# Four V-gradient stores of a decode layer go as GpSimd scatters that skip partitions 36 to 39, with those rows in a four-row SyncE store

## The chip, the cores and the metric

One core of a Trainium2 chip. The metric is device microseconds (us) of that core. A time is the median of a kernel's runs, with the lowest and highest in brackets. The span on a profile page is the profiled run's own, and is some 2 us shorter than the time of the same run. All runs of both kernels, and all timed runs of the experiments, were in the fast state, so all the comparisons below are of fast runs. One experiment (the probe) was run once, so its state is unknown, and its time is not used.

## The reference, cut to what matters

The kernel computes the forward and the backward pass of one decode layer. The layer adds, to its input, an attention over a long cache and a gated MLP.

```python
def _A_ref(x, k_cache, v_cache, wq, wo):           # x: 1 x 1 x 640
    q = transpose((x @ wq).reshape(B, Sq, 32, 128))
    scores = einsum("bhqd,bhkd->bhqk", q, k_cache) * 128 ** -0.5   # caches: 1 x 32 x 8192 x 128, bf16
    o = einsum("bhqk,bhkd->bhqd", softmax(scores), v_cache)
    return transpose(o).reshape(B, Sq, 32 * 128) @ wo
...
return x + _A_ref(layernorm(x), ...) + _B_ref(layernorm(x), ...)   # _B_ref: SwiGLU, F = 1728
# outputs: the layer's out, and the gradients of x, k_cache, v_cache, wq, wo, w1, w3, w2
```

The two caches have 67 MB each, and so have their gradients dK and dV. Everything else is small. Reading K and V and writing dK and dV is nearly all of the 303.9 MB that the core moves.

## The kernel before

A head's K or V is one 2 MB tile: 128 partitions, 16 KB in each. There are ten slots for such tiles. The gradient is written over the tile, and the tile is then stored. All loads and stores of these tiles go through one helper, on one queue, that of SyncE, which issues them in program order:

```python
dvc = out_3.rearrange("b h (p j) d -> (b h) p (j d)", p=P)     # dV, one 128-row block for each head
...
def fifo(out_, in_):                    # L102 of the profile
    nc.sync.dma_start(out_, in_)
...
free_slots = [kvpool.tile([P, KVN], BF16, name=f"kv{i}", tag=f"kv{i}") for i in range(NSLOT)]  # 10 slots
def load_next():
    if not pending or len(free_slots) < lag[0]:
        return
    kind, h = pending.pop(0)
    t = free_slots.pop(0)
    fifo(t[:], (kc if kind == "K" else vc)[h])
    kv_tiles[(kind, h)] = t
...
lag[0] = 3                              # a load goes into the slot that was stored three stores back
...
def store(kind, h):
    t = kv_tiles.pop((kind, h))
    if kind == "K":
        hd.pop(h)
    fifo((dkc if kind == "K" else dvc)[h], t[:])
    free_slots.append(t)
    load_next()
```

A load has to wait until the store that last used its slot has landed. Because the queue is in order, every wait of SyncE holds back all that stands behind it. Most of the projection weights, their gradients and those of the MLP go through the GpSimd queue, which moves 26.3 of the 303.9 MB.

## Time and profile before

| | before |
|---|---|
| time, us | 735.03 (734.04 to 735.35), 4 runs |
| span of the profiled run, us | 733.2 |
| TensorE (PE) busy | 608.6 us, 83% |
| moved | 303.90 MB, mean 414 GB/s |
| last tile store: sixteenth part lands after the fifteenth by | 8.06 us |

The page of the kernel before: busy time of the engines; DMA busy share in tenths and GB/s in 40 slices of 18.3 us; and the tile transfers with their count, size and median us from issue to landing.

```profile
PE 608.6 (83%) x5663; PEld 425.9 (58%) x5663; DVE 461.1 (63%) x806; ACT 367.9 (50%) x716; POOL 30.0 (4%) x45
...
DMA  9999999999999999999999999999999999999993
GB/s 337 401 410 420 425 428 423 400 421 422 417 422 426 429 427 424 427 430 426 429 425 428 429 420 427 429 429 427 425 428 427 428 432 428 428 431 429 422 390 154
...
out_dram<-kv SPq DMA_DIRECT2D x64, 2048.0 KB, 31.0
kv<-in_A_k_cache_dram SPq DMA_DIRECT2D x32, 2048.0 KB, 25.1
kv<-in_A_v_cache_dram SPq DMA_DIRECT2D x32, 2048.0 KB, 26.3
```

The DMA engines bound this kernel. They run at 417 to 432 GB/s in nearly every slice between the third and the last two, while the busiest compute engine is idle 17% of the time. Packet by packet, the trace shows sixteen chains ("lanes" below), one for each DMA engine. Each moves one 16 KB row after another, in 0.611 us (median), and 16 rows are in flight nearly all the time from 10 to 695 us. The table of transfers explains why: a 2 MB transfer is 4.9 us of work at 427 GB/s, yet it takes 25 to 31 us from issue to landing. So five or so transfers stand in the queue at any moment.

Busy time by stretch of the kernel before. The columns are: stretch; its length; busy us of PE, PE weight load, VectorE, ScalarE and GpSimd with their instructions in brackets; TensorE's granted clock; DMA share; GB/s.

```profile
276.00:288.00 12.00, 11.48 (x123) 8.26 (x125) 8.84 (x17) 7.89 (x17) 1.65 (x2) 0.99 1.00 421
366.00:378.00 12.00, 11.15 (x116) 7.93 (x115) 7.78 (x10) 8.06 (x16) 0.00 (x0) 1.00 1.02 425
...
544.00:556.00 12.00, 10.13 (x101) 7.16 (x101) 5.53 (x14) 7.46 (x16) 0.77 (x1) 0.86 1.00 425
715.00:720.00 5.00, 0.56 (x2) 0.50 (x2) 4.00 (x20) 0.00 (x0) 0.86 (x1) 0.50 0.84 340
...
725.00:733.00 8.00, 0.00 (x0) 0.00 (x0) 0.00 (x0) 0.00 (x0) 0.00 (x0) 0.50 0.05 23
```

In the middle of the run the DMA share is 1 (all sixteen lanes always have a packet). At the end it is not: in the last 8 us it is 0.05, which is one lane of sixteen, at 23 GB/s. A transfer lands in sixteen parts, one for each lane, and one lane has fallen behind the others by 8.06 us when the last tile store lands. That lane alone sets the end. This is the slack that the change is after. (A head's V is stored before its K, so the last store of all is dK of head 31, issued at 710.13 us. The recorded texts call it the last V store. The last V store proper is issued at 705.73, and its gap is 8.53 us in before and 4.80 in after.)

A number used below is *lost time*: the length of a stretch less the megabytes moved in it divided by 427 GB/s, the full rate. For before it is 8.05 us from 0 to 150 us (start-up), 0.25 us from 150 to 696 us, and 13.19 us from 696 us to the end.

SyncE's issues in a part of the kernel before (start; us; line and operation), and what SyncE waited for in the whole run (us in total, times, longest):

```profile
253.58 0.33 SPq L102 DMA_DIRECT2D kv<-in_A_v_cache_dram  x1
255.90 0.34 SPq L102 DMA_DIRECT2D out_dram<-kv  x1
263.62 0.33 SPq L102 DMA_DIRECT2D kv<-in_A_k_cache_dram  x1
266.96 0.34 SPq L102 DMA_DIRECT2D out_dram<-kv  x1
```

```profile
SPq L102 <- DMA out_dram<-kv: 458.2, 54, 17.1
```

SyncE waits most of the time, for stores to land, and this costs nothing: it is silent for up to 12.5 us between two issues in the middle of the run, and the queue has more work than that.

### The profile page before, as it was taken

The numbers are of one execution on the slowest core, as the hardware profiler recorded it, in microseconds if no ns is written. First come the engines' busy times: TensorE is split into PE (matmuls) and PEld (weight loads), VectorE is DVE, ScalarE is ACT, GpSimd is POOL, SyncE is SP. The second block draws the span as 40 slices with busy tenths as digits, with TensorE's granted clock in tenths as the row PEclk, the third lists the DMA queues.
The fourth block names the chain that finished last, engine by engine and source line by source line (L and its number), as shares of the span: only waits on it lengthen the run. The fifth ranks groups of instructions, "written<-read, shape, count | busy, mean of one in ns | idle before, by whom it ended". The sixth has DMA issues, their size and how long they took to land.

```text
span 733.2 us, 13850 instructions
## 1 busy us (share of the span) xinstructions
PE 608.6 (83%) x5663; PEld 425.9 (58%) x5663; DVE 461.1 (63%) x806; ACT 367.9 (50%) x716; POOL 30.0 (4%) x45
## 2 busy tenths in 40 slices
PE   1998579998899889988999797888698888899840
PEld 1666457666666666665666565555475566666520
DVE  4059655677766666667767755646746576477482
ACT  1650726665465455655565554545464455554510
POOL 0010010000100000000000000000000000000000
PEclk9996699999899889988899988989989799888965
DMA  9999999999999999999999999999999999999993
GB/s 337 401 410 420 425 428 423 400 421 422 417 422 426 429 427 424 427 430 426 429 425 428 429 420 427 429 429 427 425 428 427 428 432 428 428 431 429 422 390 154
DMA packets 27428, 303.90 MB, mean 414 GB/s; under 512 B 2836, under 2 KB 4436, under 8 KB 10724
## 3 DMA queue, kind: packets, MB, share of 16 engines
q1 hardware_dynamic: 21328, 276.39, 89.3%
q0 software_dynamic: 5728, 26.30, 8.9%
q8 instruction: 44, 0.72, 0.4%
q10 hardware_dynamic: 308, 0.33, 0.1%
q14 instruction: 20, 0.16, 0.1%
HBM read 151.67 MB, written 151.34 MB: 413 GB/s over the span
## 4 chain that ended last, share of the span: by engine, by line
PE 42%; DMA 41%; ACT 7%; DVE 7%; issue 2%; SPq 0%; ACTq 0%; DVEq 0%
PE pT L294 19%; DMA kv<-in_A_k_cache_dram 18%; DMA out_dram<-kv 17%; PE m L329 6%; PE X L406 5%; ACT KT L296 4%; DMA kv<-in_A_v_cache_dram 4%; PE sA L313 3%; PE dA L313 2%; DVE kv L439 2%; DMA wo_g<-in_A_wo_dram 2%; ACT kv L589 1%; PE gu_ps L516 1%; DVE side L240 1%; ACT KT L319 1%
## 5 line engine op out<-in xcount | busy, mean ns | idle before, releaser
L296 ACT COPY KT<-pT 128x512 f32<-128x512 f32 x512 | 290.4, 590 | 235.7 <-PE pT L294 204.3
L294 PE MATMUL pT<-ident_f,kv 128*128 128x128 f32 x2048 | 321.8, 298 | 36.5 <-DMA kv<-in_A_k_cache_dram 27.3
L294 PEld LDWEIGHTS pT<-ident_f,kv 128*128 128x128 f32 x2048 | 251.7, 156 | 93.2 <-PE pT L294 29.5
L439 DVE TENSOR_TENSOR kv<-qd,U 128x4096 bf16<-128x4096 bf16 x64 | 146.1, 2285 | 0.0
L439 DVE TENSOR_TENSOR kv<-qd,P 128x4096 bf16<-128x4096 bf16 x64 | 143.6, 2285 | 0.0
L329 PEld LDWEIGHTS m<-selc,KT 128*128 128x128 f32 x512 | 67.6, 206 | 47.1 <-ACT KT L319 37.4
L329 PE MATMUL m<-selc,KT 128*128 128x16 f32 x512 | 73.7, 277 | 24.4 <-ACT KT L319 24.2
L406 PE MATMUL X<-kv,Z 128*32 128x512 bf16 x1024 | 84.9, 460 | 1.8 <-DVE Z L423 1.8
L389 DVE SCALAR_TENSOR_TENSOR U<-m,P 128x64 bf16<-128x64 f32 x32 | 7.4, 233 | 105.4 <-PE m L329 105.4
L313 PE MATMUL sA<-KT,qz 128*32 128x512 bf16 x512 | 55.4, 423 | 0.0
L313 PE MATMUL dA<-KT,qz 128*32 128x512 bf16 x512 | 54.5, 412 | 0.2 <-ACT KT L296 0.2
L313 PEld LDWEIGHTS <-qz 128*32 128x32 bf16 x1024 | 26.5, 93 | 42.7 <-issue 41.6
L406 PEld LDWEIGHTS <-Z 128*32 128x32 bf16 x1024 | 28.7, 110 | 34.0 <-issue 17.0
L355 DVE TENSOR_REDUCE mrow<-m 128x1 f32<-128x64 f32 x32 | 7.2, 224 | 60.9 <-PE m L329 60.9
L349 ACT CAST qd<-pT 128x256 bf16<-128x256 f32 x32 | 11.9, 373 | 49.3 <-DVE kv L439 31.6
L489 DVE SCALAR_TENSOR_TENSOR wq_g<-wq_g,side 128x512 bf16<-128x512 bf16 x40 | 27.3, 683 | 0.0
L240 DVE SCALAR_TENSOR_TENSOR side<-wo_g,g_bc 128x640 bf16<-128x640 bf16 x32 | 26.2, 820 | 1.4 <-DMA wo_g<-in_A_wo_dram 1.0
L362 DVE TENSOR_REDUCE negM<-m 128x1 f32<-128x128 f32 x32 | 9.3, 292 | 25.2 <-PE m L359 25.2
L421 DVE SCALAR_TENSOR_TENSOR U<-m,P 128x128 bf16<-128x128 f32 x32 | 11.4, 355 | 19.3 <-PE m L419 19.3
L379 DVE RECIPROCAL rZ<-m 128x1 f32<-128x1 f32 x32 | 5.3, 167 | 24.2 <-PE m L373 24.2
L319 ACT COPY KT<-dA 128x512 f32<-128x512 f32 x32 | 19.4, 605 | 0.6 <-PE dA L313 0.6
L319 ACT COPY KT<-sA 128x512 f32<-128x512 f32 x32 | 19.3, 602 | 0.0
(143 smaller groups left out, 363.2 us busy)
## 6 DMA issues: line engine op xcount, KB each, us to landing
out_dram<-kv SPq DMA_DIRECT2D x64, 2048.0 KB, 31.0
kv<-in_A_k_cache_dram SPq DMA_DIRECT2D x32, 2048.0 KB, 25.1
kv<-in_A_v_cache_dram SPq DMA_DIRECT2D x32, 2048.0 KB, 26.3
out_dram<-wo_g POOLq DMA_DIRECT2D x8, 640.0 KB, 12.0
out_dram<-wq_g POOLq DMA_DIRECT2D x8, 640.0 KB, 13.0
wq_g<-in_A_wq_dram POOLq DMA_DIRECT2D x7, 640.0 KB, 13.2
wo_g<-in_A_wo_dram POOLq DMA_DIRECT2D x7, 640.0 KB, 19.5
kv<-in_B_w_dram SPq DMA_DIRECT2D x2, 1728.0 KB, 27.1
```

Source lines behind the costliest of these rows:

```text
L240: nc.vector.scalar_tensor_tensor(junk[:], G_["wo"][:, hh, :], 1.0, g_bc[:], ALU.mult, ALU.mult, accum_out=G_["do"][:, hh:hh + 1])
L294: nc.tensor.transpose(pT[:, k * P:(k + 1) * P], W3[:, 4 * c + k, :], ident_f[:])
L296: nc.scalar.copy(KT[:].rearrange("p k w -> p (k w)"), pT[:])
L313: nc.tensor.matmul(S_[kind][q:q + QW, :], lhsT=S_["qz"][:, o:o + QW], rhs=KTb[:, par, :], start=(c0 == 0), stop=(c0 == NCH - 2), skip_grou ...
L319: nc.scalar.copy(XS[:].rearrange("p k w -> p (k w)"), S_.pop(kind)[:])
L329: nc.tensor.matmul(S_["m"][:, b0:b0 + J].rearrange("p (c k t) -> p k c t", k=4, t=2)[:, k, :, :], lhsT=XS[:, k, :], rhs=selc[:].rearrange( ...
L349: nc.scalar.copy(qd[:].rearrange("p a d -> p (a d)"), hd[h].pop("ps_r"))
L362: nc.vector.tensor_reduce(S_["negM"][:], S_["m"][:, 2 * J:2 * J + P], AX.X, ALU.max, negate=True)
L406: nc.tensor.matmul(xg["X"][q:q + QW, :], lhsT=Z[:, o:o + QW], rhs=W[:, N4 * i:N4 * (i + 1)], start=(slot == 0 and i < 4), stop=(slot == NS ...
L421: nc.vector.scalar_tensor_tensor(S_["U2"][:], S_["V"][:, 0:J].unsqueeze(2).to_broadcast([P, J, 2]), S_["m"][:, OC + NS:OC + NS + 1], S_["P ...
L439: nc.vector.tensor_tensor(dst[:, lo * DH:hi * DH].rearrange("p (j a b) -> p j a b", a=DH // 2, b=2), vec.rearrange("p (a b) -> p a b", b=2 ...
L489: nc.vector.scalar_tensor_tensor(wq_g[:, ci, :], wq_g[:, ci, :], 1.0, dqb, ALU.mult, ALU.mult, accum_out=dxa[:, ci, g:g + 1])
```

## The change

Its intent: the late lane gets less work. Four V stores (heads 9, 13, 17 and 21) are issued by GpSimd as scatters by row index. The index of partitions 36 to 39 is pushed out of bounds, so these rows are skipped. They follow as a small store of four rows on the SyncE queue.

```diff
+    SCAT = (9, 13, 17, 21)
+    R0, NR = 36, 4
+    dvc_rows = out_3.rearrange("b h (p j) d -> (b h p) (j d)", p=P)
+    sidx = masks[:, 4:8].bitcast(mybir.dt.int32)
+    nc.gpsimd.iota(sidx, pattern=[[(SCAT[1] - SCAT[0]) * P, len(SCAT)]], base=SCAT[0] * P, channel_multiplier=1)
+    skip = ln3[:, 3:4]
+    nc.vector.tensor_reduce(skip, ident_f[:, R0:R0 + NR], AX.X, ALU.add)
+    nc.vector.scalar_tensor_tensor(sidx, skip.to_broadcast([P, len(SCAT)]), float(2 * H * P), sidx,
+                                   ALU.mult, ALU.add)
 ...
     def store(kind, h):
 ...
-        fifo((dkc if kind == "K" else dvc)[h], t[:])
+        dst = (dkc if kind == "K" else dvc)[h]
+        if kind == "V" and h in SCAT:
+            i = SCAT.index(h)
+            nc.gpsimd.indirect_dma_start(
+                out=dvc_rows, out_offset=bass.IndirectOffsetOnAxis(ap=sidx[:, i:i + 1], axis=0),
+                in_=t[:], in_offset=None, bounds_check=H * P - 1, oob_is_err=False)
+            fifo(dst[R0:R0 + NR], t[R0:R0 + NR])
+        else:
+            fifo(dst, t[:])
```

(The tile `masks` grows from 4 to 8 columns and `ln3` from 3 to 4, to hold the index and the marker.)

The diff does not say one thing, which the built order shows. The scatter names the whole of dV as its output. So it has to wait until the V store ahead of it has landed, and the four-row store has to wait until the scatter has landed. The second wait stands in the SyncE queue.

More of the change, by code (lines that the diff above doesn't have):

```diff
@@ L162 @@
     nc.vector.tensor_copy(ident_bf[:], ident_f[:])
-    masks = consts.tile([P, 4], F32, name="masks")
+    masks = consts.tile([P, 8], F32, name="masks")
     pm_one = masks[:, 0:2]
@@ L209, in pst @@
         return ps_t.tile([P, 512], F32, name="pT", tag="pT")
-    ln3 = consts.tile([P, 3], F32, name="ln3")
+    ln3 = consts.tile([P, 4], F32, name="ln3")
     msum, sumsq, std = ln3[:, 0:1], ln3[:, 1:2], ln3[:, 2:3]
```

## The prediction

> **What bounds the kernel now.** The DMA engines. The busy-by-stretch view gives a DMA share of 1.00 to 1.01 at 418 to 428 GB/s from 50 to 700 us; the page has PE at 83%, POOL at 4%. Packet by packet, the trace shows 16 in flight from 10 to 695 us: each of 16 lanes moves one 16 KB row after another in 0.611 us. Only the lanes' total work and the tail count.
>
> The tail is unbalanced. Each 2 MB transfer lands in 16 parts, one a lane. The last lane trails the fifteenth by about 1.5 us near 150 us, 3 near 400, 6 near 660 and 8.1 at the last V store (724.2 against 732.2). From 725.8 to 731.8 us one lane alone is busy. It sets the end; the span is 733.2.
>
> **What the change does.** It seems meant to relieve that lane: four stores lose four rows on one lane, which go as a four-row store. The Trainium skill ("DMA: Bandwidth & Descriptors", "The descriptor swizzle") puts partitions 36 to 39 on engine 1; its section on semaphore increments puts a four-row SyncE transfer on the lowest four engines. Then engine 1 loses 3 rows net a store: 12 x 0.611 = 7.3 us. If the indexed path deals rows otherwise, the relieved lane can lie outside the lowest four and lose 16 rows, 9.8 us. The trace names no engine; that the relieved lane is the late one is my main assumption (3 in 4). The other low lanes gain 4 rows, 2.4 us, within the 8 us of slack.
>
> **New waits.** In the built order the scatter counts as a write to the whole output: it waits for earlier V stores to land, and the four-row store waits on the SyncE queue for the scatter to land. Estimated from the trace: at the first (near 255 us) the previous V store lands at 263.5; a GpSimd transfer's first packet comes 4.2 us after issue; eight 16 KB packets a lane, alternating with the other queue's, take 8 x 1.22 = 9.8 us; so it lands about 279, and SyncE issues nothing for 25 us, four times. But SyncE then has four or five transfers of 4.9 us outstanding (each 25 to 34 us in flight), which the scatter's bytes stretch, so the lanes should just stay fed. I allow 0 to 1 us lost each time. GpSimd's issue[...] and the index operations are off the path.
>
> **Sum.** 735.0 - 7 to 8 (the next lane is 8 us ahead) + 0 to 3 = about 729 us. Range 725 to 737, its upper part for a relieved lane that isn't the late one, or lanes that run dry.
>
> **What would show it.** Right: the last V store's sixteenth landing within 3 us of the fifteenth; no one-lane stretch at the end; DMA share still 1.0 near 255, 340, 430 and 515 us; SyncE waits of 20 to 30 us on a scatter's landing, without longer PE waits on loads. Wrong: the same 8 us gap; dips of GB/s at the four stores; a scatter landing far later than 16 us after issue.
>
> **What would make it wrong.** Smaller packets in the indexed path, or slow index handling on GpSimd; SyncE's silence draining the lanes; another lane nearly as late.
>
> Chances: faster by over 2% 0.03, within 2% 0.91, slower by over 2% 0.06.

## The result and the profile after

| | before | after |
|---|---|---|
| time, us | 735.03 (734.04 to 735.35), 4 runs | 742.61 (742.51 to 743.64), 4 runs |
| span of the profiled run, us | 733.2 | 740.7 |
| lost time 0 to 150 us | 8.05 | 6.59 |
| lost time 150 to 696 us | 0.25 | 15.32 |
| lost time 696 us to the end | 13.19 | 7.07 |
| sixteenth part of the last tile store after the fifteenth | 8.06 | 4.71 |

The ratio is 1.0112, 95% interval 1.0097 to 1.0127: the kernel became 1.1% slower. Ratios here and below are the mean time of one kernel's runs over that of the other's in the same rounds, so they are not quite the ratio of the quoted medians. The prediction was 729.0 with a range of 725 to 737, so the result lies outside it.

The three rows of lost time add up to the change of the span: 15.32 - 0.25 in the middle, less 13.19 - 7.07 at the end, less 8.05 - 6.59 in the start-up, is 7.49 us; the spans differ by 7.5. The last of the three is scatter: in these two and the eleven other profiled runs that were read for it, the start-up lost between 6.4 and 8.4 us, with no order by kernel.

The page of the kernel after:

```profile
PE 598.4 (81%) x5663; PEld 418.9 (57%) x5663; DVE 459.8 (62%) x808; ACT 368.2 (50%) x716; POOL 35.4 (5%) x50
...
DMA  8999999999999999999999999999999999999996
GB/s 334 405 410 422 425 419 430 425 428 426 424 424 428 426 413 334 423 430 428 395 391 424 430 427 355 406 427 430 429 345 416 430 429 429 427 430 427 428 430 253
...
out_dram<-kv SPq DMA_DIRECT2D x60, 2048.0 KB, 29.5
kv<-in_A_k_cache_dram SPq DMA_DIRECT2D x32, 2048.0 KB, 17.1
kv<-in_A_v_cache_dram SPq DMA_DIRECT2D x32, 2048.0 KB, 28.2
```

GB/s has four dips (334; 395 and 391; 355; 345), and its last slice is better, 253 in place of 154. The tenths in the DMA row hide the dips. K loads now land 17.1 us after issue, in place of 25.1: the queue ahead of them is shorter.

Busy time by stretch, the same middle stretches as before, then the new end:

```profile
276.00:288.00 12.00, 11.15 (x114) 8.12 (x106) 7.41 (x8) 7.84 (x16) 0.33 (x1) 1.00 0.84 271
366.00:378.00 12.00, 5.67 (x33) 4.66 (x34) 0.67 (x2) 2.56 (x5) 1.64 (x2) 0.57 0.95 333
...
544.00:556.00 12.00, 6.76 (x34) 5.55 (x35) 0.36 (x2) 2.90 (x5) 1.65 (x2) 0.51 0.92 308
725.00:730.00 5.00, 0.93 (x3) 0.59 (x3) 3.19 (x16) 0.00 (x0) 0.86 (x1) 0.50 0.99 423
730.00:735.00 5.00, 0.00 (x0) 0.00 (x0) 0.00 (x0) 0.00 (x0) 0.00 (x0) 0.50 0.62 257
735.00:740.00 5.00, 0.00 (x0) 0.00 (x0) 0.00 (x0) 0.00 (x0) 0.00 (x0) 0.50 0.05 19
```

In these stretches the rate falls from 421 and 425 GB/s to between 271 and 333. Yet the DMA share falls only to 0.84 to 0.95. Between 22 and 36% of the rate is gone, but the lanes are idle for only 5 to 16% of the time. So there are two parts to a dip: lanes with nothing to do, and lanes whose packets take longer. TensorE's busy time falls by a third to a half in the two later ones, because its loads come late: from 366 to 378 us it waits 7.8 us for one V load, where in the same stretch of before its longest wait is 0.8 us.

SyncE's issues around the first scatter, what SyncE waited for, and the scatters with their time from issue to landing:

```profile
251.76 0.33 SPq L102 DMA_DIRECT2D kv<-in_A_v_cache_dram  x1
279.13 0.34 SPq L102 DMA_DIRECT2D out_dram<-kv  x1
279.58 0.35 SPq L102 DMA_DIRECT2D kv<-in_A_k_cache_dram  x1
279.99 1.61 SPq L102 DMA_DIRECT2D out_dram<-kv  x1
281.70 1.36 SPq L102 DMA_DIRECT2D kv<-in_A_v_cache_dram  x1
283.11 0.69 SPq L102 DMA_DIRECT2D out_dram<-kv  x1
283.91 0.84 SPq L102 DMA_DIRECT2D kv<-in_A_k_cache_dram  x1
284.80 0.63 SPq L102 DMA_DIRECT2D out_dram<-kv  x1
```

```profile
SPq L102 <- DMA out_dram<-kv: 374.7, 45, 16.8
SPq L102 <- DMA out_dram<-kv,masks: 106.0, 4, 27.0
```

```profile
L467 POOL DMA_INDIRECT out_dram<-kv,masks x4: 1048/1373/1453, 262.6 to 528.7; - x4
...
DMA to landing us min/median/max: 15.6/16.1/16.4
```

The chain of events at the first scatter: SyncE issues a V load at 251.76. Its next instruction is the four-row store. GpSimd waits for the V store ahead to land (261.65), issues the scatter at 262.63, and this lands at 279.07. Only then does SyncE go on, at 279.13, after 27.4 us of silence, and it issues seven transfers in 5.7 us. The four waits on a scatter (out_dram<-kv,masks) sum to 106.0 us.

What the lanes did meanwhile is in the packets. The V load of 251.76, the last work that SyncE queued before the silence, landed in sixteen parts, one a lane:

```
273.5 273.71 273.74 274.07 274.61 275.06 276.46 277.82 278.24 278.37 278.8 279.01 279.85 280.87 281.0 283.1
```

Twelve of the sixteen lanes had finished it before SyncE spoke again. They still had their share of the scatter, up to 279.07 at most, and then nothing. Here are GB/s and the mean number of lanes with a packet in flight, for each us from 274 on:

```
us      274 275 276  277  278  279 280 281  282  283  284 285  286
GB/s    428 410 370  281  242  153 147 240  291  349  266 230  264
lanes  16  15.8 14.2 10.6 9.3  6.1 9.3 15.5 13.7 15.4 16  15.7 16
```

There are two troughs. From 276 to 281 lanes stand idle. From 284 to 287 they are all busy, and the rate is still only about 250 GB/s. Busy time by stretch, first of before and then of after, shows the second trough on its own:

```profile
284.00:287.00 3.00, 2.48 (x40) 1.95 (x40) 2.90 (x7) 1.41 (x4) 0.00 (x0) 1.00 1.01 416
```

```profile
278.00:281.00 3.00, 3.00 (x37) 2.08 (x36) 1.69 (x5) 1.17 (x2) 0.00 (x0) 1.00 0.76 212
284.00:287.00 3.00, 3.00 (x29) 2.16 (x27) 2.70 (x2) 2.58 (x6) 0.00 (x0) 1.00 0.96 243
```

With a share of 0.96, after moved 243 GB/s where before moved 416: a 16 KB packet takes 0.611 us at other times. Of the 44 that began here, 13 took 0.61 to 0.65 us, 12 up to 1 us, and 19 took 1 to 2.07 us.

Summed over the four dips (lost in stretches of about 30 us around each: 4.69, 2.90, 3.92 and 3.60 us, together 15.1), empty lanes account for 2.05, 0.70, 1.42 and 1.14 us for each lane, together 5.3. The remaining 9.8 us or so is slow packets.

### The profile page after: what moved, and what is told of

It reads as the page before. It is cut to its first block, busy times and chain, and to the rows that moved or that the text cites. A ratio compares the mean times of both kernels' runs of the same rounds, so it can differ in the third digit from the quotient of the medians.

```text
span 740.7 us, 13878 instructions
## 1 busy us (share of the span) xinstructions
PE 598.4 (81%) x5663; PEld 418.9 (57%) x5663; DVE 459.8 (62%) x808; ACT 368.2 (50%) x716; POOL 35.4 (5%) x50
## 4 chain that ended last, share of the span: by engine, by line
DMA 44%; PE 39%; ACT 7%; DVE 6%; issue 2%; SPq 0%; ACTq 0%; DVEq 0%; POOLq 0%
PE pT L304 18%; DMA kv<-in_A_k_cache_dram 16%; DMA out_dram<-kv 13%; DMA kv<-in_A_v_cache_dram 12%; PE m L339 5%; ACT KT L306 4%; PE X L416 4%; PE sA L323 3%; PE dA L323 2%; DMA out_dram<-kv,masks 2%; DVE kv L449 2%; DMA wo_g<-in_A_wo_dram 2%; ACT kv L607 1%; PE gu_ps L534 1%; DVE side L240 1%
## 5 line engine op out<-in xcount | busy, mean ns | idle before, releaser
L304 PE MATMUL pT<-ident_f,kv 128*128 128x128 f32 x2048 | 318.0, 296 | 62.6 <-DMA kv<-in_A_k_cache_dram 34.5
L304 PEld LDWEIGHTS pT<-ident_f,kv 128*128 128x128 f32 x2048 | 246.7, 153 | 118.7 <-issue 45.6
L339 PEld LDWEIGHTS m<-selc,KT 128*128 128x128 f32 x512 | 65.5, 200 | 39.4 <-ACT KT L329 29.3
L339 PE MATMUL m<-selc,KT 128*128 128x16 f32 x512 | 71.0, 271 | 17.8 <-ACT KT L329 17.5
L416 PE MATMUL X<-kv,Z 128*32 128x512 bf16 x1024 | 80.5, 441 | 1.8 <-DVE Z L433 1.8
L323 PE MATMUL dA<-KT,qz 128*32 128x512 bf16 x512 | 56.8, 430 | 0.2 <-ACT KT L306 0.2
L323 PEld LDWEIGHTS <-qz 128*32 128x32 bf16 x1024 | 26.7, 94 | 42.7 <-issue 41.5
L416 PEld LDWEIGHTS <-Z 128*32 128x32 bf16 x1024 | 27.4, 107 | 32.3 <-issue 13.6
## 6 DMA issues: line engine op xcount, KB each, us to landing
kv<-in_A_k_cache_dram SPq DMA_DIRECT2D x32, 2048.0 KB, 17.1
kv<-in_B_w_dram SPq DMA_DIRECT2D x2, 1728.0 KB, 27.1
```

The costliest lines, as they stand in the source:

```text
L304: nc.tensor.transpose(pT[:, k * P:(k + 1) * P], W3[:, 4 * c + k, :], ident_f[:])
L323: nc.tensor.matmul(S_[kind][q:q + QW, :], lhsT=S_["qz"][:, o:o + QW], rhs=KTb[:, par, :], start=(c0 == 0), stop=(c0 == NCH - 2), skip_grou ...
L339: nc.tensor.matmul(S_["m"][:, b0:b0 + J].rearrange("p (c k t) -> p k c t", k=4, t=2)[:, k, :, :], lhsT=XS[:, k, :], rhs=selc[:].rearrange( ...
L416: nc.tensor.matmul(xg["X"][q:q + QW, :], lhsT=Z[:, o:o + QW], rhs=W[:, N4 * i:N4 * (i + 1)], start=(slot == 0 and i < 4), stop=(slot == NS ...
```

## The experiments

My theory after the comparison (T1): the time is lost because SyncE's silence on the scatter's landing lets the queue run dry. The rivals: (T2) the scatter itself is dear, through its index handling or its descriptors; (T3) the relief of one lane fails, and the end gap only moved by chance. A second question was whether rows 36 to 39 lie on the late lane at all. Twelve kernels were run. All gave correct results.

| run | time, us | ratio to before [95%] | longest silences of SyncE, us | lost 150 to 696 | lost 696 to end | end gap |
|---|---|---|---|---|---|---|
| before | 735.03 | 1 | up to 12.5 | 0.25 | 13.19 | 8.06 |
| after | 742.61 | 1.0112 [1.0097, 1.0127] | 27.4, 27.0, 26.5, 26.7 | 15.32 | 7.07 | 4.71 |
| late4 | 738.99 | 1.0079 [1.0062, 1.0096] | 20.9, 21.6, 22.0, 20.5 | 6.68 | 9.35 | 6.66 |
| noskip | 742.0 | 1.0107 [1.0091, 1.0124] | 26.0, 27.6, 28.1, 27.1 | 15.84 | 6.56 | 4.09 |
| late_all | 735.64 | 1.003 [1.0014, 1.0047] | up to 15.5 | 0.40 | 13.51 | 7.74 |
| hold | 734.38 | 1.0011 [0.9995, 1.0028] | 12.8 | 1.08 | 12.29 | 7.82 |
| act4 | 736.72 | 1.0031 [1.0005, 1.0057] | 14.1 to 16.4 | 2.08 | 14.42 | 10.56 |
| dup4 | 753.3 | 1.0253 [1.0236, 1.0271] | 34.6, 33.4, 33.0, 34.2 | 30.10 | 4.59 | 0.25 |
| act4_r16 | 729.76 | 0.994 [0.9919, 0.9962] | 13.6 to 16.2 | 1.23 | 7.42 | 0.76 |
| act4_r48 | 730.01 | 0.9941 [0.9923, 0.996] | up to 15.1 | 1.99 | 7.95 | 2.22 |
| after_r16 | 741.41 | 1.0097 [1.0074, 1.0121] | 26.4, 27.1, 26.9, 27.0 | 12.89 | 5.47 | 0.95 |
| pool_dup | 734.06 | 1.0003 [0.9985, 1.0021] | 15.9 | 0.55 | 12.23 | 7.76 |
| pool_dup2 | 735.91 | 1.002 [1.0003, 1.0036] | 24.0 once, then up to 14.7 | 2.44 | 10.43 | 3.97 |

"End gap" is the time between the fifteenth and the sixteenth landing of the last tile store.

### late4: the four rows one head later, the scatter's output narrowed

```diff
-                out=dvc_rows, out_offset=...
-                in_=t[:], in_offset=None, bounds_check=H * P - 1, oob_is_err=False)
-            fifo(dst[R0:R0 + NR], t[R0:R0 + NR])
+                out=dvc_rows[0:(h + 1) * P], out_offset=...
+                in_=t[:], in_offset=None, bounds_check=(h + 1) * P - 1, oob_is_err=False)
+            late_rows.append((dst, t))
         else:
             fifo(dst, t[:])
+        if kind == "V" and h - 1 in SCAT:
+            d4, t4 = late_rows.pop()
+            fifo(d4[R0:R0 + NR], t4[R0:R0 + NR])
```

> The same four scatters with the same skipped rows, but the four-row store goes on the SyncE queue one V store later (when the scatter has landed) and the scatter's declared output ends with its own head, so that later V stores don't wait for it. Theory A (the loss is SyncE's silence: the lanes run dry and then restart slowly; the relief itself works): SyncE waits on a scatter vanish, no dips of GB/s at the four places, the last V store's sixteenth landing within 4 us of the fifteenth, time 727 to 731 us. Rival B (the scatter costs by itself, by slower packets or by GpSimd's work on indices): dips stay, 738 us or more. Rival C (partitions 36 to 39 are not on the late lane): no dips, gap of 7 us or more at the end, 734 to 738 us.

Measured: 738.99 us (737.71 to 740.81), still about 70% of the slowdown (0.79% of 1.12%). By its numbers this is the outcome written for rival B, and the forecast for T1 (theory A there) missed. The four dips became smaller and moved about 20 us later. SyncE in late4:

```profile
278.79 0.33 SPq L102 DMA_DIRECT2D kv<-in_A_v_cache_dram  x1
279.21 1.73 SPq L102 DMA_DIRECT2D out_dram<-kv  x2
301.51 0.36 SPq L102 DMA_DIRECT2D kv<-in_A_k_cache_dram  x1
```

The wait on the scatter is gone, and a new one took its place. The last four-row store is issued at about 280.6, behind some 20 us of queued work, and lands at 301.46. The slot that it reads is the one that the next load wants, so SyncE is silent until 301.51. A tiny store lands no sooner than the queue ahead of it. So the dips stand where the new silences are and not where the scatters are, which fits T1 better than B, but late4 was not the clean test that I meant it to be. Its 6.68 us are nearly all slow packets: empty lanes account for about 1.3 us of them.

### noskip: all 128 rows scattered, every wait kept

```diff
-    nc.vector.tensor_reduce(skip, ident_f[:, R0:R0 + NR], AX.X, ALU.add)
+    nc.vector.memset(skip, 0.0)
```

> The change with one part undone: the scatters move all 128 rows (no index out of bounds), the four-row store follows as before and writes the same four rows again, so all waits stay. If the skipped rows are on the late lane: the gap between fifteenth and sixteenth landing at the end is some us larger than in the changed kernel (4.7 us there) and the time 745 to 750 us. If they are not, or if the relief is worth nothing beside the dips: 742 to 744 us and the same gap.

The four-row store then writes the same rows a second time. Measured: 742.0 us, the same as after, and an end gap of 4.09 against 4.71. So the skipped rows are worth nothing in this change (within about 1 us), and the smaller gap at the end is not their doing. The dips themselves level the lanes: at a tile load that lands near 590 us, after the last dip, the sixteenth part trails the fifteenth by 0.5 us in after and 0.0 in noskip, and by 4.0 in before.

### late_all: the scatter alone, without skip and without four-row store

```diff
     (late4, and)
-    nc.vector.tensor_reduce(skip, ident_f[:, R0:R0 + NR], AX.X, ALU.add)
+    nc.vector.memset(skip, 0.0)
-            fifo(d4[R0:R0 + NR], t4[R0:R0 + NR])
```

> Scatters of all 128 rows, no four-row store, no wait of SyncE on a scatter: the GpSimd path alone, without relief. Theory A: as the kernel before, 734 to 737 us, end gap about 8 us. Rival B (the scatter costs by itself): 738 us or more. Against the first run of this call it gives the worth of the relief without the dips.

Measured: 735.64 us, 0.3% over before, 0.40 us lost in the middle. The scatters still take their index path. T2 is refuted as an explanation of the 1.1%; what the scatters themselves may cost is about 0.3% (0.14 to 0.47).

### hold: stores of four heads moved to the next head's first store (on before)

```diff
+        if h in SCAT:
+            held.append((kind, h))
+            return
+        while held:
+            store_now(*held.pop(0))
+        store_now(kind, h)
```

> The kernel before, no scatter, the same bytes on the same queues; only that at heads 9, 13, 17 and 21 the V and K stores and the loads behind them are issued one head later, so that SyncE issues nothing for some 23 us and then five or six transfers at once. Theory A: dips like the changed kernel's (a dry trough and a second, slow one, 3 to 4.5 us lost each), 10 to 15 us lost, part given back in the tail since the dips level the lanes: 741 to 748 us. Rival B (slow packets come from the scatter): only the dry trough, about 1.3 us each, 734 to 738 us.

Measured: 734.38 us. This was meant to make silence without a scatter, and it made none: its longest gap between two issues was 12.8 us. A look at the trace shows why: the loads moved along with the stores, so the 137 issues of SyncE stand in the same order as in before, and each goes out when its own data and slot are ready. The experiment says nothing about T1. It was replaced by dup4.

### dup4: silence without any scatter (on before)

```diff
+        dst = (dkc if kind == "K" else dvc)[h]
+        fifo(dst, t[:])
+        if kind == "V" and h in (9, 13, 17, 21):
+            fifo(dst[36:40], t[36:40])
```

> The kernel before, no GpSimd store and no skipped rows: at heads 9, 13, 17 and 21 SyncE issues its V store and then writes four of its rows again, which waits for that store to land, so SyncE is silent for some 30 us and the lanes drain. Theory A (silence that outlasts the queued work is the loss, whatever causes it): four dips of 3 to 6 us each, the lanes levelled at each, 743 to 755 us, end gap under 5.5 us. Rival B (the loss needs the scatter or its shared queue): under 738 us.

The four rows are written twice to the same place, so SyncE waits until the full store has landed. Measured: 753.3 us, 2.5% slower, silences of 33 to 35 us and 30.1 us lost in the middle. GB/s in 40 slices, then SyncE's longest wait, in dup4:

```profile
GB/s 341 401 410 423 422 427 427 420 423 428 416 412 427 427 410 246 429 430 427 407 298 431 423 422 368 346 428 425 408 335 372 428 428 429 427 427 426 423 429 318
...
SPq L102 <- DMA out_dram<-kv: 484.4, 45, 33.8
```

There is no scatter, no index and no GpSimd store in it, and it has the same four dips, deeper. Longer silence, more loss. Empty lanes account for 18.0 us of the 30.1 (6.2, 3.8, 3.9 and 4.2 for each lane); about 12 are again packets that run slow after the silence. T1 holds. T2 is not needed. (The loss at each dip, 7.5 us, is more than the 3 to 6 us that I had expected.) And the end gap, 0.25 us, came without any skipped row, as T1 with noskip says.

### probe: which engine is the late one? (on before)

```diff
         fifo((dkc if kind == "K" else dvc)[h], t[:])
+        if kind == "V" and 14 <= h < 30:
+            k = h - 13
+            fifo(probe_t[0:k, h - 14:h - 13], probe_src[0:k, 0:1])
```

> The kernel before with 16 tiny SyncE loads behind V stores of heads 14 to 29, of 1, 2, ... 16 rows, which by the Trainium skill run on the lowest-numbered 1, 2, ... 16 engines. Each lane's part lands when that lane has done its share of the store ahead, so the landings show where those lanes stand among the 16 of that store. Expected: the first four stand in the middle or ahead (as in the runs before); from some k on one part lands with the last of the store ahead, 4 to 7 us late: that k less 1 is the number of the late lane, and I expect it above 3. Time as before within 1%.

After the V stores of heads 14 to 29 a tiny load of k rows follows, k from 1 to 16. The Trainium skill ("DMA: Bandwidth & Descriptors", "Why a DMA increments its semaphore by 16 and not by 1") says that a SyncE transfer of k rows, k up to 16, runs on the lowest-numbered k engines. A part of the probe stands behind its lane's share of the store, so it lands late when the late lane is among the k.

```
k=4   probe parts land 448.03 448.35 451.97 452.38                  the store ahead: 447.64 ... 457.51 459.65
k=5   probe parts land 468.95 469.23 472.37 472.64 481.33           the store ahead: 468.77 ... 478.48 481.14
```

With k = 4 no part is late. With k = 5 and every larger k, the last part lands with the store's last. So the fifth engine, number 4, is the late one. The number of landings agrees with the page's rule. The same skill page ("The descriptor swizzle") puts partitions 16 to 19 and 48 to 51 on engine 4, and 36 to 39 on engine 1. The change relieves engine 1. Nothing in the runs tells why engine 4 is late, but it is not a trait of one chip: the record has the probe on chip 12, and act4_r16 and act4_r48 below, which find the same engine late, on chip 5.

### act4: no silence, rows 36 to 39

```diff
+            nc.scalar.dma_start(dst[R0:R0 + NR], t[R0:R0 + NR])
             nc.gpsimd.indirect_dma_start(
-                out=dvc_rows, out_offset=...
-                in_=t[:], in_offset=None, bounds_check=H * P - 1, oob_is_err=False)
-            fifo(dst[R0:R0 + NR], t[R0:R0 + NR])
+                out=dvc_rows[0:(h + 1) * P], out_offset=...
+                in_=t[:], in_offset=None, bounds_check=(h + 1) * P - 1, oob_is_err=False)
```

> The change with the same scatters and skipped rows 36 to 39, but the four rows go first, from the ScalarE queue, and the scatter's declared output ends with its own head: nothing on SyncE waits for a scatter but the load into that slot. No dips expected. Theory D (36 to 39 are on a lane of the lowest four, which isn't late): 734 to 737 us, last V store's sixteenth landing 7 to 8.5 us behind the fifteenth. Rival E (the rows are on the late lane, and only the dips hid it): 726 to 731 us, gap under 3 us.

The four rows go first, and on ScalarE's queue, so SyncE waits for no scatter. Measured: 736.72 us (734.95 to 738.66), 2.08 us lost in the middle, no dips, and an end gap of 10.56 us. Time and dips are as theory D says; the gap is above its 7 to 8.5 us, and I cannot say why. The skip does thin one lane: at the first scatter fifteen lanes moved eight of its 16 KB rows and one moved four. It is not the lane that ends last.

### act4_r16 and act4_r48: no silence, rows of engine 4

```diff
     (act4, and)
-    R0, NR = 36, 4
+    R0, NR = 16, 4          # act4_r16;  48, 4 in act4_r48
```

> As act4, only that the four skipped rows are 16 to 19 in place of 36 to 39. The probe put the late lane at engine 4; by the Trainium skill's descriptor swizzle that is partitions 16 to 19 and 48 to 51. Theory D (the change relieves the wrong lane): 16 rows of 0.611 us, 9.8 us, come off the late lane; the sixteenth landing of the last V store within 3 us of the fifteenth, no lane alone at the end, 726 to 731 us. Rival F (the scatter deals rows out by another map, or a lane's lateness isn't worth its rows): as act4, 735 to 738 us, gap 7 us or more.

> As act4_r16 with rows 48 to 51, the other four rows that the swizzle puts on engine 4. Theory D with the swizzle's map: the same as act4_r16 within 2 us. If rows go to lanes by another map (eight neighbours to a lane, for example), the two differ, and one of them is as act4.

Measured: 729.76 us (726.3 to 731.69, 6 runs), ratio 0.994, and 730.01 us, ratio 0.9941. These beat both kernels. The end gap is 0.76 and 2.22 us. Busy time by stretch at the end of act4_r16:

```profile
715.00:720.00 5.00, 0.93 (x3) 0.58 (x3) 1.12 (x5) 0.00 (x0) 0.17 (x1) 0.50 0.79 325
720.00:726.00 6.00, 0.00 (x0) 0.00 (x0) 0.00 (x0) 0.00 (x0) 0.00 (x0) 0.50 0.16 66
```

There is no stretch of one lonely lane any more. The right rows are worth 1.0031 - 0.9940 = 0.9% of before, 6.7 us, and the lost time at the end says the same: 14.42 - 7.42 = 7.0 us. Two different blocks of four rows, 16 to 19 and 48 to 51, do the same, as the swizzle of the skill page says they should. That page speaks of plain 128-partition transfers; the runs show the scatter by index following the same map.

### after_r16: the change with the rows of engine 4

```diff
-    R0, NR = 36, 4
+    R0, NR = 16, 4
```

> The changed kernel word for word, only R0 = 16 in place of 36: the right lane by theory D, with SyncE's waits on the scatter kept. Theory G (at each wait the lanes drain and start level again, so what a lane was spared before is lost; only what builds up after the last dip, near 550 us, is left): 740 to 744 us, dips and end gap as in the changed kernel, 4 to 5 us. Rival (the spared rows count in spite of the dips): 733 to 738 us.

Measured: 741.41 us (738.6 to 742.69), ratio 1.0097. The same relief that is worth 6.7 us without dips is worth about 1.1 us (1.0112 - 1.0097, and the intervals overlap) with them. The loss in the middle stays, 12.89 us. The end gap of 0.95 is smaller than the 4 to 5 us that I had expected; probably another lane came last, but the trace does not name the lanes, so this is not shown. T3 is half right: in this change the relief does fail, but only because it is aimed at another lane (act4_r16), and the dips swallow most of what the right lane gains. It cannot explain a loss in the middle.

### pool_dup and pool_dup2: how long a silence is free? (on before)

```diff
+        if kind == "V" and h in (9, 13, 17, 21):
+            nc.gpsimd.dma_start(dst, t[:])
+            nc.gpsimd.dma_start(dst[36:40], t[36:40])     # pool_dup2 only
+            fifo(dst[36:40], t[36:40])
+        else:
+            fifo(dst, t[:])
```

> The kernel before, with the four V stores as plain GpSimd stores of all 128 rows, and the four rows written again by SyncE, which waits for the GpSimd store to land. The plain store declares only its own head, so it doesn't wait for the V store before it, and SyncE should be silent for 10 to 18 us in place of 27: less than the queued work lasts. Theory A (only silence that outlasts the queue costs; the slow packets follow from lanes run dry): no dips, 734 to 737 us, 16 packets in flight throughout. Rival H (any wait on the landing followed by several transfers at once slows the packets): slow packets, 2 us or more lost at each of the four, 739 us or more.

> As pool_dup, with one more link in the chain: the four rows are written by GpSimd again after its store has landed, and SyncE's four rows wait for that, so SyncE should be silent for some 18 to 23 us (pool_dup: 11.5 us and free; the changed kernel: 27 us and not free), then issue three to five transfers close together. If slow packets need lanes that have run dry: lanes fed throughout, 733 to 736 us, no stretch under 400 GB/s. If the burst of issues alone slows packets: 16 in flight all the time but stretches at 200 to 350 GB/s after each wait, 737 us or more. If the lanes run dry already at this length, that shows as fewer than 16 in flight and it decides nothing about the burst.

These store the whole tile by a plain GpSimd transfer, to have silences of other lengths. Measured: 734.06 us, ratio 1.0003, silences of up to 15.9 us, nothing lost, as theory A had it; rival H is refuted. In pool_dup2 (735.91 us, 1.002) the first place has a silence of 24.0 us, and the others about 14 us with at most 0.4 us lost at each. The first place of pool_dup2, SyncE and then busy time by stretch:

```profile
253.65 0.33 SPq L102 DMA_DIRECT2D kv<-in_A_v_cache_dram  x1
277.64 0.34 SPq L102 DMA_DIRECT2D out_dram<-kv  x1
278.09 0.35 SPq L102 DMA_DIRECT2D kv<-in_A_k_cache_dram  x1
278.50 1.82 SPq L102 DMA_DIRECT2D out_dram<-kv  x1
```

```profile
275.00:278.00 3.00, 3.00 (x24) 2.07 (x23) 3.00 (x2) 1.96 (x4) 0.00 (x0) 0.83 1.03 437
278.00:281.00 3.00, 3.00 (x27) 2.36 (x26) 1.09 (x3) 2.43 (x5) 0.00 (x0) 1.00 0.95 348
281.00:284.00 3.00, 2.94 (x27) 2.04 (x27) 1.77 (x5) 2.18 (x6) 0.00 (x0) 1.00 1.05 352
```

The lanes were still full when SyncE spoke again (1.03), and were empty for only 0.17 us each. Yet 1.7 us were lost right after, at a share of about 1 and 350 GB/s. So the slow packets do not need lanes that stand idle for long. They follow a burst of issues into a queue that has nearly run out.

Is it the burst or the short queue? Two traces separate them. In pool_dup SyncE issues a V load, a store, a K load and a store within 1.4 us, from 454.97 on, after a silence of 12 us. In late4 it issues the same kinds of transfer within 1.4 us, from 301.51 on, after one of 21 us. Busy time by stretch, first of pool_dup and then of late4:

```profile
454.00:470.00 16.00, 15.79 (x173) 11.10 (x171) 11.57 (x17) 10.81 (x23) 0.00 (x0) 1.00 1.02 432
```

```profile
300.00:316.00 16.00, 14.87 (x153) 10.28 (x152) 9.91 (x20) 8.96 (x19) 0.76 (x1) 0.91 0.98 374
```

What SyncE had issued and the lanes had not yet begun to move was 3.3 MB in pool_dup and 0.55 MB in late4 when the burst began. In the 15 us around each burst, the four of pool_dup (2.8 to 4.5 MB) lost 0.3 us or less; the four of late4 (0.2 to 0.55 MB) lost 1.4 to 2.0 us, and that of pool_dup2 (0.85 MB) 1.7 us. So a burst of four transfers is free by itself, and the slow packets need the short queue, or the longer silence that goes with it. Whether a short queue without a burst would do it, no run shows.

Put together: silences up to 16 us cost little (0.55 us lost in the whole middle of pool_dup, 1.2 to 2.1 us in act4 and its two variants), those of 20.5 to 22 us cost 1.7 us each in late4 (6.68 / 4), the one of 24.0 us cost 1.7 us, those of 26 to 28 us cost 2.9 to 4.7 us each in after, and those of 33 to 35 us cost 7.5 us each in dup4 (30.1 / 4).

## Why the prediction was wrong

- **What bounds the kernel: right.** The DMA lanes, with a free tail of one lane. act4_r16 recovers 6.7 us from that tail, near the prediction's 7 to 8. The agreement is in part luck: the prediction took 12 rows off the lane (7.3 us), act4_r16 takes 16 (9.8 us).
- **The waits: right.** It foresaw the scatter's wait for the store ahead, the four-row store's wait for the scatter, a landing 15.5 us after the issue (279 less 263.5; measured 15.6 to 16.4), and 25 us of silence four times (measured waits 106.0 us in all, 26.5 each).
- **What the silence costs: wrong, and this is the step that failed.** The prediction put it so: "so the lanes should just stay fed. I allow 0 to 1 us lost each time". Measured: 2.90 to 4.69 us each, 15.1 us in all, where the sum had 0 to 3. Two things were missed. First, the size: the prediction compared the silence with the whole queue, up to the landing of its last part. For the V load of 251.76 that last part did land late, at 283.1. But that is one lane; twelve of sixteen lanes had landed theirs before 279.1, and the first at 273.5. Lanes spread over 9.6 us leave the early ones with that much less queued work. The empty lanes are 5.3 of the 15.1 us. Second, the way back: the prediction had no term for a slow restart, and the runs show one, the other 9.8 us. That it follows the silence is shown (dup4, pool_dup2), and that it needs a queue that has nearly run out (late4 beside pool_dup); its inner cause is not.
- **Which lane: wrong.** "That the relieved lane is the late one is my main assumption (3 in 4)." The late lane is engine 4 (probe, act4_r16, act4_r48); the change thins another (act4), by the skill's map engine 1. By itself this would have left the time near that of act4, 736.7 us, inside the range. In the change as it stands it makes hardly a difference: noskip and after_r16 both stay within about 1 us of it.
- **The tail: its size nearly right, for another reason.** The end lost 6.1 us less than before (13.19 - 7.07), but noskip, which skips nothing, has the same gain (6.56 lost). The dips level the lanes. After the last dip the gap grew again, to 4.7 us by the end.
- **Interleaving of the queues: right.** The Trainium skill ("DMA: Bandwidth & Descriptors", "Issuing engines are not separate DMA queues") says that transfers of all issuing engines share the same sixteen DMA engines. late_all and pool_dup agree: moving four stores to GpSimd changes the time by 0.3% and 0.03%.

What stays open: why engine 4 is late; why packets are slow after a queue has nearly run out; the end gap of act4; and the 0.3% of late_all and act4.

## What to carry to other kernels

In these runs a wait in the in-order DMA queue was free when 2.8 MB or more were still queued at its end (pool_dup), and not when 0.85 MB or less were, even with nearly all lanes still fed (late4, pool_dup2). So size a wait against the first part of the last transfer to land, not the last part, leave a margin, and allow for a slow restart. Before relieving a late DMA engine, find out which one it is (tiny transfers of k rows do it), and check that the relief doesn't bring a new wait: a write by index counts as a write to all that its output names, so name the narrowest range and put the dependent small store ahead of it, on another queue. Done that way, with the right rows, the same idea gives 729.8 us in place of 742.6.

## What the Trainium skill lacked or had wrong

- "DMA: Bandwidth & Descriptors", "Latency and other measured facts", says that DMA engines 7 and 15 are usually the slower ones, and ties this to GpSimd's transfers. Here, where 276.4 of the 303.9 MB go through SyncE's queue, it was engine 4, 8.06 us behind at the end of before; why, no run shows.
- The same page, "Specifications", gives about 358 GB/s as the HBM limit of a core. Before holds 417 to 432 GB/s (reads and writes together, each transfer counted once) for over 600 us. The fabric ceiling of 435 GB/s in the same table fits. The page is not wrong as a whole: its section "Bandwidth" says that the lower figure is for both cores of a pair streaming, and lists 425 GB/s for one core alone, as here; the row in "Specifications" doesn't say so.
- The same section gives about 1 us to the first byte of a GpSimd transfer. With the lanes loaded, its first packet came 4.2 us (3.3 to 4.4) after the start of the issue in before, and that of the four scatters 4.6 to 4.9 us in after.
- No page says that the rate stays low after a queue has nearly run out and is refilled at once: 243 GB/s for 3 us with nearly all lanes busy in after, and SyncE's own issues at 0.63 to 1.61 us, in place of 0.33.
- No page says how rows skipped by an index out of bounds spread over the engines: the scatter kept the plain map, so four neighbouring rows came off one engine alone (four rows in place of eight).
